# A linear-attention layer and a balanced mixture of experts: u spread over the partitions by TensorE, and one expert's second weights issued later

## The chip, the cores and the metric

The kernel runs on one core of one Trainium2 chip. The metric is the device time of one execution in microseconds; lower is better. The kernel before takes 377.23 us (median of 3 runs, 376.42 to 378.08).

## The reference, cut to what matters

All data is float32. The first half is an attention with a decaying state (4 batches, 8 heads, 768 steps, 48 channels):

```python
for t in range(S):
    kt, vt, rt = k[:, :, t], v[:, :, t], r[:, :, t]
    cur = einsum('bhd,bhe->bhde', u[None] * kt, vt)
    y[:, :, t] = einsum('bhd,bhde->bhe', rt, state + cur)
    state = w[None, :, :, None] * state + einsum('bhd,bhe->bhde', kt, vt)
```

`u` and `w` hold 8 x 48 values; `u` weighs the step's own key and value. The outputs are laid out as 3072 rows of 384. The second half gives each row to one of 8 experts: all (row, expert) scores are sorted, and each expert takes its best 384 rows that are still free. Then, for each expert e,

```python
h = maximum(x[mask] @ w1[e], 0.0)      # w1[e]: 384 x 1024
out[mask] = h @ w2[e]                  # w2[e]: 1024 x 384
```

## The kernel before

The attention works in 24 units of 128 steps of one batch (unit n is chunk n // 4 of batch n % 4). Class `Mild` does it, and its method `run` issues everything in an order written out by hand; each engine executes its own part of that order, one instruction after the other, and waits on semaphores where data is missing. For a unit, TensorE turns keys and r (`keys_turned`, `r_turned`, from unit 2 on `turn`), VectorE scales them with powers of w (table W), TensorE multiplies keys with r (`pairs`, g_ps), and VectorE copies the masked result over a diagonal (AT). The diagonal holds the sum over channels of r·k·u: GpSimd multiplies r with k (`own_raw`, L435) and by u (`own_rest`, L440), VectorE sums (`own_sum`, dd, L444), ScalarE and VectorE put dd on the diagonals (`diagonal`). So u is needed with its 384 values on each of the 128 partitions, as u_bc. `outputs` then makes the unit's result, which is turned to rows and written to the internal tensor x_rows (L621) two units later.

Nearly all loads are issued by SyncE, in the order of the program, and go through one queue: in `start` w, keys and r of unit 0, u as a broadcast from memory to all partitions (L353), then keys, r and v of the next units. `idle` issues turnings of the identity that nobody reads.

While the last units run, one expert (the "star") is chosen from the chunks that are done, and its first 256 rows are listed among the first 20 units. The generator `walk.early` does this in eleven steps, and the list `steps` says at which place of which unit each is taken. Its third step, in unit 18, knows the expert and calls `on_star`, which loads both of its weight matrices; its tenth, in the middle of unit 23, has the row numbers (e_tok) and calls `on_tokens`, which issues two gathers of 128 rows from x_rows by GpSimd (L1531). A gather waits until the rows of units 0 to 19 have landed in memory.

After the last unit TensorE turns the gathered rows (e_xT_ps, L1898), multiplies them with w1 (e_h_ps, L1906) and later with w2 (e_o_ps, L1915). Between these products the choice of the next expert goes on: VectorE makes masks (ind) and TensorE counts with them (counts). The other experts follow, each with weights, gather, two products and a scatter, with a search for the next between.

Names in the rows: krs are keys and r of a unit (loaded from in_k_dram and in_r_dram), vts its v, kT_ps and rT_ps keys and r turned, krT the scaled ones, rk the product of r and k, xr a unit's rows before they are written, w the weights of an expert, xg gathered rows, spare_ps a free bank of PSUM.

Of the kernel before, what the change touches and what calls it, by code (L numbers as in the profile page):

```python
# [10 lines left out]
F32 = mybir.dt.float32  # L11
# [265 lines left out]
class Mild:  # L277
# [30 lines left out]
    def open(self, ctx):  # L308
        tc, HP, H, D, B = self.tc, self.HP, self.H, self.D, self.B
        const = self.const = ctx.enter_context(tc.tile_pool(name="m_const", bufs=1))  # L310
        self.pool = ctx.enter_context(tc.tile_pool(name="m_work", bufs=2))
        self.xpool = ctx.enter_context(tc.tile_pool(name="m_x", bufs=1))
        self.ps = ctx.enter_context(tc.tile_pool(name="m_ps", bufs=1, space=PSUM))
        self.NK, self.NV, self.NS = 5, 6, 3
        self.krs = const.tile([128, self.NK, 2, H, PD], F32, name="krs")
        self.vts = const.tile([128, self.NV, H, PD], F32, name="vts")
        self.kss = const.tile([128, self.NS, H, PD], F32, name="kss")
        self.states = const.tile([128, B, HP, PD], F32, name="states")
        self.wp = const.tile([128, HP], F32, name="wp")
        self.wc = const.tile([128, HP], F32, name="wc")  # L320
        self.ones8 = const.tile([128, 2, 2, HP, 9], F32, name="ones8")
        self.times = const.tile([128, HP, 9], F32, name="times")
        self.begin = const.tile([128, HP, 9], F32, name="begin")
        self.Q = const.tile([128, 2, HP, 9, 8], F32, name="Q")
        self.chunk = const.tile([128, HP], F32, name="chunk")
        self.W = const.tile([128, 2, HP, T], F32, name="W")
        self.WK, self.WR = self.W[:, 0], self.W[:, 1]
        self.wk = const.tile([128, H, D], F32, name="wk")
        self.u_bc = const.tile([128, H, D], F32, name="u_bc")
        self.wgp = const.tile([128, HP, 32], F32, name="wgp")  # L330
        self.mask_f = const.tile([128, T], F32, name="mask_f")
        self.mask = const.tile([128, T], U8, name="mask")
        self.bad = const.tile([128, HP], BF16, name="bad")
        self.xts, self.live, self.lgs, self.unscaled = {}, {}, {}, []

    def load(self, n, what):
        if n >= self.N:
            return
        nc, H, D = self.nc, self.H, self.D
        b, c = self.units[n]  # L340
        for x in what:
            t = self.vts[:, n % self.NV] if x == "v" else self.krs[:, n % self.NK, "kr".index(x)]
            src = {"k": self.k, "r": self.r, "v": self.v}[x]
            nc.sync.dma_start(t[:, :, 0:D], src[b, :, ts(c, T), :].rearrange("h s d -> s h d"))

    def start(self):
        nc, HP, H, D = self.nc, self.HP, self.H, self.D
        nc.vector.memset(self.wp, 1.0)
        with nc.allow_non_contiguous_dma(reason="a row to the partitions"):
            for z, eng in enumerate((nc.sync, nc.scalar)):  # L350
                eng.dma_start(self.wp[z * PD:z * PD + D, :], self.w[z:H:2].rearrange("h d -> d h"))
        self.load(0, "kr")
        nc.sync.dma_start(self.u_bc.rearrange("p h d -> p (h d)"), self.u.rearrange("h d -> (h d)").partition_broadcast(128))  # L353
        for n, what in ((1, "kr"), (0, "v"), (2, "kr"), (1, "v"), (3, "kr"), (2, "v"), (4, "kr"), (3, "v")):
            self.load(n, what)
        make_identity(nc, self.ident)
        nc.vector.memset(self.krs[:, :, :, :, D:PD], 0.0)
        AB = self.ones8
        nc.vector.memset(self.times[:, :, 0:1], 0.0)
        nc.vector.memset(self.begin, 0.0)  # L360
        nc.vector.memset(self.begin[:, :, 0:1], 1.0)
        nc.gpsimd.memset(self.wgp, 0.0)
        nc.scalar.copy(self.bad, self.ident[:, 0:HP])
        self.spare = self.ps.tile([128, 2, 512], F32, name="spare_ps", tag="y_ps")
        self.idle(12, self.spare[:, 1])

        nc.gpsimd.memset(self.mask_f, 1.0)
        nc.gpsimd.affine_select(out=self.mask_f, in_=self.mask_f, compare_op=ALU.is_ge, fill=0.0, base=-1,
                                pattern=[[1, T]], channel_multiplier=-1)
        nc.gpsimd.memset(self.kss[:, :, :, D:PD], 0.0)  # L370
        nc.gpsimd.memset(self.vts[:, :, :, D:PD], 0.0)
        nc.gpsimd.memset(self.states[:, :, :, D:PD], 0.0)
        nc.gpsimd.tensor_copy(self.mask, self.mask_f)


        def powers(i):
            nc.vector.tensor_tensor_scan(out=AB[:, 0, i].rearrange("p a j -> p (a j)"),
                                         data0=self.times.rearrange("p a j -> p (a j)"),
                                         data1=self.begin.rearrange("p a j -> p (a j)"),
                                         initial=0.0, op0=ALU.mult, op1=ALU.add)  # L380

        each = self.times[:, :, 1:9]
        nc.vector.tensor_scalar(out=each, in0=self.wp.unsqueeze(2).to_broadcast([128, HP, 8]), scalar1=W_MIN,
                                scalar2=W_MAX, op0=ALU.max, op1=ALU.min)
        powers(0)
        nc.vector.tensor_copy(each, AB[:, 0, 0, :, 8:9].to_broadcast([128, HP, 8]))
        powers(1)
        nc.vector.reciprocal(AB[:, 1], AB[:, 0])
        for x, eng in ((0, nc.gpsimd), (1, nc.vector)):
            eng.tensor_mul(self.Q[:, x], AB[:, x, 1].unsqueeze(3).to_broadcast([128, HP, 9, 8]),  # L390
                           AB[:, x, 0, :, 0:8].unsqueeze(2).to_broadcast([128, HP, 9, 8]))
        self.own_raw(0)
        Q = self.Q.rearrange("p x a i j -> p x a (i j)")
        M = PD
        self.pieces = {"k": ((slice(0, M + 1), Q[:, 0, :, M::-1]), (slice(M + 1, T), Q[:, 1, :, 1:T - M])),
                       "r": ((slice(0, M + 2), Q[:, 1, :, M + 1::-1]), (slice(M + 2, T), Q[:, 0, :, 1:T - M - 1]))}

    def gate_weights(self):
        wg = self.wg.rearrange("(i j z d) e -> i z d j e", i=2, z=2, d=self.D)
        for q in range(2):  # L400
            for i in range(2):
                self.nc.sync.dma_start(self.wgp[q * PD:q * PD + self.D, 2 * i:2 * i + 2, 0:self.E],
                                       wg[i, 1 - q if i else q])

    def idle(self, m, ps):
        if isinstance(ps, str):
# [234 lines left out]
    def run(self, step):  # L641
        N, B, C, walk = self.N, self.B, self.C, self.walk
        self.live = {n: {} for n in range(N)}
        self.start()
        k0 = self.keys_turned(0, True)
        r0 = self.r_turned(0)
        self.own_rest(0)
        self.scaled(0, "k", k0, "pieces")
# [2 lines left out]
        self.table(self.WR, "r")  # L651
        self.own_sum(0)
        self.diagonal(0, (1,), self.spare[:, 1, 0:T])
        self.idle(2, "g_ps")
        k1 = self.keys_turned(1, True, walk.ps, "few")
        self.scaled(1, "k", k1, self.WK)
        self.pairs(0)
# [5 lines left out]
        nc, AB = self.nc, self.ones8  # L663
# [80 lines left out]
        last = self.rows_turned((N - 1,), "g_ps")  # L744
# [720 lines left out]
def rwkv5_eagle_then_base_layer_balanced(  # L1465
# [12 lines left out]
    nc = tc.nc  # L1478
# [21 lines left out]
    class Experts:  # L1500
# [11 lines left out]
            self.first = pool("f_first", 1, **how)  # L1512
            self.ps_t, self.ps_h, self.ps_o = (pool(f"f_ps_{x}", 2, space=PSUM, **how) for x in "tho")

        def load_weights(self, n, fmax):
            number = walk.outs.tile([1, 1], I32, name="number")
            nc.vector.tensor_scalar(out=number, in0=fmax[0:1, :], scalar1=1.0, scalar2=float(E),
                                    op0=ALU.max, op1=ALU.min)
            pool = self.turns[n % 2]
            w1, w2 = pool.tile([128, KD, F], F32, name="w1"), pool.tile([128, KF, DX], F32, name="w2")  # L1520
            e = nc.values_load(number[0:1, 0:1], engines=(mybir.EngineType.SP,), min_val=1, max_val=E,
                               skip_runtime_bounds_check_because="held between 1 and E")
            for t, src in ((w2, moe_w2), (w1, moe_w1)):
                nc.sync.dma_start(t, src[ds(E - e, 1)].rearrange("o (c p) f -> p (o c) f", p=128))
            return w1, w2

        def gather(self, n, tok, within=N):
# [395 lines left out]
    with ExitStack() as whole:  # L1923
        x = Experts()
# [3 lines left out]
        have = {}  # L1928
        first = walk.new_outs()
        with ExitStack() as part:  # L1930
# [2 lines left out]
            epool = part.enter_context(tc.tile_pool(name="f_early", bufs=1))  # L1933

            def on_star(star):
                have["w"] = x.load_weights(0, star)

            def on_tokens(tok):
                have["x"] = x.gather(0, tok, N - N // C), tok
# [2 lines left out]
            U = mild.N  # L1942
# [4 lines left out]
            def step(n, at):  # L1947
                for _ in range(steps.count((n, at))):
                    next(early)

            with tc.manual_schedule():
                one, last = mild.run(step)
# [24 lines left out]
                second = walk.new_outs()  # L1977
# [55 lines left out]
    with tc.If(have["ok"] < 1, label="whole", preferred_fallthrough_block=False):  # L2033
# [3 lines left out]
        with ExitStack() as arm:  # L2037
            x = Experts()
# [40 lines left out]
```

## Time and profile before

| | |
|---|---|
| median of 3 runs | 377.23 us (376.42 to 378.08) |
| the profiled execution | 378.76 us |
| its span, first to last instruction | 377.0 us |
| mean granted TensorE clock | 0.998 |
| TensorE busy (matmul / weight load) | 96% / 79% of the span |
| VectorE, ScalarE, GpSimd busy | 75%, 47%, 36% |
| moved by DMA | 60.74 MB, 161 GB/s on average |

The rows further down come from this profiled execution. Its span and the 1.76 us around it make its time. A busy TensorE is not one at its peak, and time in which an engine stands still matters only where something behind it is late for that reason.

### The profile page before, as it was taken

The numbers are of one execution on the slowest core, as the hardware profiler recorded it, in microseconds if no ns is written. First come the engines' busy times: TensorE is split into PE (matmuls) and PEld (weight loads), VectorE is DVE, ScalarE is ACT, GpSimd is POOL, SyncE is SP. The second block draws the span as 40 slices with busy tenths as digits, with TensorE's granted clock in tenths as the row PEclk, the third lists the DMA queues.
The fourth block names the chain that finished last, engine by engine and source line by source line (L and its number), as shares of the span: only waits on it lengthen the run. The fifth ranks groups of instructions, "written<-read, shape, count | busy, mean of one in ns | idle before, by whom it ended". The sixth has DMA issues, their size and how long they took to land.

```text
span 377.0 us, 10330 instructions
## 1 busy us (share of the span) xinstructions
PE 360.3 (96%) x4008; PEld 298.7 (79%) x4008; DVE 283.1 (75%) x945; ACT 177.2 (47%) x457; POOL 136.8 (36%) x169
## 2 busy tenths in 40 slices
PE   6889999999998999999999999999999999999994
PEld 5678888888786757587997898559657889989994
DVE  5888899789984677976978869877367964995640
ACT  3787878888753202234435444321222535535230
POOL 6898987787402041212112121103203422060031
PEclk9999999999999999999999999999999999999999
DMA  6998878888793091825646463109109574590110
GB/s 127 196 185 192 188 170 188 191 182 184 207 325 108 12 383 45 314 87 103 229 190 107 155 265 83 43 7 367 67 23 324 156 252 188 81 381 23 24 64 29
DMA packets 108234, 60.74 MB, mean 161 GB/s; under 512 B 90000, under 2 KB 102416, under 8 KB 108176
## 3 DMA queue, kind: packets, MB, share of 16 engines
q1 hardware_dynamic: 104896, 50.55, 49.3%
q0 software_dynamic: 3072, 9.44, 7.1%
q8 instruction: 33, 0.54, 0.7%
q14 instruction: 25, 0.20, 0.2%
q10 hardware_dynamic: 208, 0.00, 0.0%
HBM read 47.40 MB, written 9.44 MB: 151 GB/s over the span
## 4 chain that ended last, share of the span: by engine, by line
PE 51%; DMA 17%; issue 15%; DVE 11%; POOL 3%; SPq 2%; POOLq 0%; ACT 0%; DVEq 0%
DMA out_dram<-o_all,to 9%; PE y_ps L556 6%; PE o_ps L1801 6%; PE h_ps L1656 5%; PE pa_ps L1730 5%; PE g_ps L516 4%; PE h_ps L1633 4%; PE hb_ps L1633 3%; DMA xg<-x_rows,tok 3%; DMA w<-in_moe_w_dram 3%; PE e_h_ps L1906 3%; DVE AT L523 2%; PE kr_ps L488 2%; PE kv_ps L535 2%; DVE krT L492 2%
## 5 line engine op out<-in xcount | busy, mean ns | idle before, releaser
L506 ACT ACTIVATE AT<-ident,dd 128x128 f32<-128x128 f32 x188 | 58.3, 394 | 6.4 <-DVE dd L444 6.4
L1656 PE MATMUL h_ps<-xT,w 128*128 128x384 f32 (+1 forms) x216 | 56.3, 412 | 0.5 <-ACT xT L1547 0.5
L1785 POOL DMA_INDIRECT out_dram<-o_all,to x16 | 21.5, 1346 | 89.8 <-DVE o_all L1773 41.0
L1531 POOL DMA_INDIRECT xg<-x_rows,tok x22 | 22.3, 1015 | 85.1 <-DVE own_c L1457 31.6
L1656 PEld LDWEIGHTS h_ps<-xT,w 128*128 128x128 f32 x216 | 33.3, 191 | 14.4 <-issue 1.3
L523 DVE COPY_PREDICATED AT<-mask,g_ps 64x512 f32<-64x512 uint8 (+1 forms) x48 | 32.4, 725 | 3.5 <-PE g_ps L516 1.5
L1659 ACT ACTIVATE hid<-h_ps 128x384 f32<-128x384 f32 (+1 forms) x32 | 14.0, 437 | 42.7 <-PE h_ps L1656 41.0
L492 DVE TENSOR_TENSOR krT<-kr_ps,W 112x512 f32<-112x512 f32 x44 | 28.1, 679 | 3.3 <-PE kr_ps L488 3.3
L435 POOL TENSOR_TENSOR rk<-krs 128x384 f32<-128x384 f32 x24 | 24.3, 1012 | 13.9 <-DMA krs<-in_r_dram 6.5
L1801 PE MATMUL o_ps<-w,hid 128*128 128x384 f32 x80 | 28.0, 491 | 0.0
L516 PE MATMUL g_ps<-krT 48*64 48x128 f32 (+1 forms) x768 | 26.3, 255 | 1.7 <-DVE AT L523 1.0
L556 PE MATMUL y_ps<-AT,vts 128*64 128x128 f32 x384 | 25.7, 276 | 0.0
L440 POOL TENSOR_TENSOR rk<-rk,u_bc 128x384 f32<-128x384 f32 x24 | 24.2, 1007 | 3.1 <-DMA u_bc<-in_u_dram 1.3
L516 PEld LDWEIGHTS g_ps<-krT 48*64 48x64 f32 x768 | 20.6, 132 | 3.7 <-PE kv_ps L535 1.1
L556 PEld LDWEIGHTS y_ps<-AT,vts 128*64 128x64 f32 x384 | 20.6, 137 | 1.1 <-issue 0.9
L1621 ACT ACTIVATE hid<-kept_P 128x384 f32<-128x384 f32 x24 | 12.6, 523 | 17.4 <-DVE kept_P L1625 17.1
L1801 PEld LDWEIGHTS o_ps<-w,hid 128*128 128x128 f32 x80 | 14.5, 190 | 7.7 <-issue 0.4
L426 POOL TENSOR_TENSOR kss<-krs,wk 128x384 f32<-128x384 f32 x20 | 20.3, 1017 | 0.0
L620 ACT COPY xr<-x_ps 128x192 f32<-128x192 f32 x48 | 12.9, 324 | 8.0 <-PE x_ps L606 3.8
L575 ACT COPY x<-y_ps 128x512 f32<-128x512 f32 x24 | 14.0, 583 | 4.3 <-PE y_ps L556 3.6
L556 PE MATMUL y_ps<-krT,states 48*64 48x128 f32 x320 | 15.8, 278 | 0.2 <-ACT x L575 0.2
L488 PE MATMUL kr_ps<-ident,krs 64*112 64x64 f32 x352 | 15.0, 223 | 0.9 <-DVE krT L492 0.3
(337 smaller groups left out, 838.1 us busy)
## 6 DMA issues: line engine op xcount, KB each, us to landing
w<-in_moe_w_dram SPq DMA_DIRECT2D x18, 1536.0 KB, 9.2
krs<-in_k_dram SPq DMA_DIRECT2D x24, 192.0 KB, 4.2
krs<-in_r_dram SPq DMA_DIRECT2D x24, 192.0 KB, 4.4
vts<-in_v_dram SPq DMA_DIRECT2D x24, 192.0 KB, 4.8
x_rows<-xr SPq DMA_DIRECT2D x24, 192.0 KB, 4.3
xg<-x_rows,tok POOLq DMA_INDIRECT x22, 5.3
xg<-xg SPq DMA_TRANSPOSE x16, 3.4
out_dram<-o_all,to POOLq DMA_INDIRECT x16, 3.3
```

The costliest lines, as they stand in the source:

```text
L435: nc.gpsimd.tensor_mul(rk, self.krs[:, n % self.NK, 1, :, 0:D], self.krs[:, n % self.NK, 0, :, 0:D])
L440: self.nc.gpsimd.tensor_mul(rk, rk, self.u_bc)
L488: nc.tensor.transpose(ps[0:P, x, a, :], self.pair(kr[:, x], a)[rows], self.ident[rows, rows])
L492: nc.vector.tensor_mul(t[0:P, :, :, ts(i, PD)], ps[0:P], self.W[0:P, :, :, ts(i, PD)])
L506: nc.scalar.mul(AT[:, z, a, :], self.ident, dd[:, h:h + 1])
L516: nc.tensor.matmul(g_ps[ts(i, PD), z, a, i * PD:], kT[rows, a, ts(i, PD)], rT[rows, a, i * PD:], start=True, stop=True)
L523: nc.vector.copy_predicated(out=AT[keys, :, :, steps], mask=mask, data=g_ps[keys, :, :, steps])
L556: nc.tensor.matmul(yv[q * PD:(q + 1) * PD, o // 2, o % 2, :], lhsT, rhs, start=(o // 2, q) not in seen, stop=stop, skip_group_check=True)
L1531: self.gathered = nc.gpsimd.indirect_dma_start(out=xg[:, c, :], out_offset=None, in_=x_dram[0:within, :], in_offset=bass.IndirectOffsetOnA ...
L1633: nc.tensor.matmul(ps[:, q, :], w[b][:, ts(p * Q + q, 128)], x[a], start=fresh, stop=(a, b) == pairs[-1], skip_group_check=True)
L1656: nc.tensor.matmul(h_ps[j][:, at], w1[:, f, ts(j, 128)], xT[:, f, at], start=(f == 0), stop=(f == KD - 1))
L1801: nc.tensor.matmul(o_ps, hid[:, j, ts(c, 128)], w2[:, j, :], start=(j == 0), stop=(j == KF - 1))
```

## The change

Two things are changed.

u no longer comes as a broadcast from memory. ScalarE's queue loads it as a column tile u_col of 128 x 3 values. `spread_u` then issues three turnings on TensorE: its operand is one column of u_col, read 128 times by a step of zero, so that each turning puts 128 values of u on all partitions. ScalarE copies the 384 columns from PSUM to u_bc. The turnings stand between the keys and the r of unit 0. Two unread turnings a little later are left out.

The star's weights are no longer loaded together. `on_star` loads w1 alone; w2 is issued in unit 23 after the last of the eleven steps, so that in the program it stands behind the two gathers. All other experts load w2 and then w1, as before.

```diff
@@ start @@
-        self.load(0, "kr")
-        nc.sync.dma_start(self.u_bc.rearrange("p h d -> p (h d)"), self.u.rearrange("h d -> (h d)").partition_broadcast(128))
-        for n, what in ((1, "kr"), (0, "v"), (2, "kr"), (1, "v"), (3, "kr"), (2, "v"), (4, "kr"), (3, "v")):
+            nc.scalar.dma_start(self.u_col, self.u.rearrange("h d -> (h d)").rearrange("(c p) -> p c", p=128))
+        for n, what in ((0, "kr"), (1, "kr"), (0, "v"), (2, "kr"), (1, "v"), (3, "kr"), (2, "v"), (4, "kr"), (3, "v")):
             self.load(n, what)
...
+    def spread_u(self):
+        nc, ps = self.nc, self.spare[:, 0, 0:self.H * self.D]
+        for c in range(self.H * self.D // 128):
+            nc.tensor.transpose(ps[:, ts(c, 128)], self.u_col[:, c:c + 1].to_broadcast([128, 128]), self.ident)
+        nc.scalar.copy(self.u_bc.rearrange("p h d -> p (h d)"), ps)
@@ run @@
         k0 = self.keys_turned(0, True)
+        self.spread_u()
         r0 = self.r_turned(0)
...
         self.diagonal(0, (1,), self.spare[:, 1, 0:T])
-        self.idle(2, "g_ps")
         k1 = self.keys_turned(1, True, walk.ps, "few")
@@ load_weights @@
-            for t, src in ((w2, moe_w2), (w1, moe_w1)):
+            def load(t, src):
                 nc.sync.dma_start(t, src[ds(E - e, 1)].rearrange("o (c p) f -> p (o c) f", p=128))
+            if later:
+                load(w1, moe_w1)
+                return w1, w2, lambda: load(w2, moe_w2)
+            load(w2, moe_w2)
+            load(w1, moe_w1)
             return w1, w2
@@ on_star, step @@
-                have["w"] = x.load_weights(0, star)
+                *have["w"], have["second"] = x.load_weights(0, star, later=True)
...
                 for _ in range(steps.count((n, at))):
                     next(early)
+                if (n, at) == (U - 1, "last"):
+                    have["second"]()
```

How the order of instructions changes, at two places. First TensorE at the start of the program, before (spare_ps here takes the unread turnings; kT_ps and rT_ps are those of unit 0, then of unit 1):

```order
L409 MATMUL spare_ps_186<-ident_58 128x128 x12
L453 MATMUL kT_ps_214<-ident_58,krs_135 112x128 x4
L453 MATMUL rT_ps_219<-ident_58,krs_135 112x128 x4
L409 MATMUL unread_ps_242<-ident_58 128x128 x2
L453 MATMUL kT_ps_245<-ident_58,krs_135 112x128 x4
```

and TensorE at the same place now:

```order
L415 MATMUL spare_ps_187<-ident_58 128x128 x12
L459 MATMUL kT_ps_215<-ident_58,krs_135 112x128 x4
L408 MATMUL spare_ps_187<-ident_58,u_col_149 128x128 x3
L459 MATMUL rT_ps_224<-ident_58,krs_135 112x128 x4
L459 MATMUL kT_ps_247<-ident_58,krs_135 112x128 x4
```

The three turnings of u stand before those of r(0), and the two unread ones are gone.

Second SyncE from unit 18 on, before, from the rows of unit 16 on (w2 and w1 are the star's weights, the five transfers from xr_2366 on are those of units 17 to 21):

```order
L621 DMA x_rows<-xr_2252 128x384
L1521 TENSOR_LOAD number_2293
L1524 ISA
L1524 DMA w2_2296<-in_moe_w2_dram 128x8x384
L1524 ISA
L1524 DMA w1_2295<-in_moe_w1_dram 128x3x1024
L344 DMA vts_136<-in_v_dram 128x8x48
L621 DMA x_rows<-xr_2366 128x384
L621 DMA x_rows<-xr_2470 128x384
L621 DMA x_rows<-xr_2589 128x384
L621 DMA x_rows<-xr_2669 128x384
L621 DMA x_rows<-xr_2732 128x384
```

and SyncE at the same place now:

```order
L1530 DMA w1_2297<-in_moe_w1_dram 128x3x1024
L345 DMA vts_136<-in_v_dram 128x8x48
L627 DMA x_rows<-xr_2367 128x384
L627 DMA x_rows<-xr_2471 128x384
L627 DMA x_rows<-xr_2590 128x384
L627 DMA x_rows<-xr_2670 128x384
L627 DMA x_rows<-xr_2733 128x384
L1530 ISA
L1530 DMA w2_2298<-in_moe_w2_dram 128x8x384
L627 DMA x_rows<-xr_2812 128x384
L627 DMA x_rows<-xr_2816 128x384
```

w2 has moved behind the rows of unit 21 and ahead of those of the last two units.

## Rows read from the trace of the kernel before

**Rows 1.** The page's chain of waits, by engine: share of the span.

```profile
PE 51%; DMA 17%; issue 15%; DVE 11%; POOL 3%; SPq 2%; POOLq 0%; ACT 0%; DVEq 0%
```

**Rows 2.** Timeline of GpSimd, 4 to 9 us: start us, us, instruction, [idle before it, releaser].

```profile
5.44 1.03 POOL L435 TENSOR_TENSOR rk<-krs 128x384 f32<-128x384 f32 x1 [0.51 <-DMA krs<-in_r_dram]
7.75 1.00 POOL L440 TENSOR_TENSOR rk<-rk,u_bc 128x384 f32<-128x384 f32 x1 [1.28 <-DMA u_bc<-in_u_dram]
```

**Rows 3.** Timeline of SyncE at the start: the load of u.

```profile
2.54 0.72 SPq L353 DMA_DIRECT2D u_bc<-in_u_dram  x1
```

**Rows 4.** DMA issues in two stretches at the start: KB each, us to landing.

```profile
wp<-in_w_dram ACTq DMA_DIRECT2D x1, 0.8 KB, 2.2
...
u_bc<-in_u_dram SPq DMA_DIRECT2D x1, 192.0 KB, 5.1
```

**Rows 5.** Timeline of VectorE, 4 to 10 us.

```profile
6.49 0.76 DVE L468 TENSOR_TENSOR krT<-rT_ps,Q 112x264 f32<-112x264 f32 x2 [0.23 <-PE rT_ps L453]
8.78 0.55 DVE L444 TENSOR_REDUCE dd<-rk 128x8 f32<-128x384 f32 x1 [1.54 <-POOL rk L440]
```

**Rows 6.** Timeline of TensorE's matmuls, 1 to 13 us.

```profile
4.32 1.07 PE L453 MATMUL kT_ps<-ident,krs 128*112 128x128 f32 x4
5.35 1.10 PE L453 MATMUL rT_ps<-ident,krs 128*112 128x128 f32 x4
...
8.40 0.66 PE L453 MATMUL kT_ps<-ident,krs 128*112 128x128 f32 x4 [1.52 <-DMA krs<-in_k_dram]
```

**Rows 7.** Chain of waits, 0 to 32 us: start us, us, what.

```profile
8.34 3.72 DMA krs<-in_r_dram
...
16.33 1.00 POOL rk L440
```

**Rows 8.** Chain of waits, 111.9 to 119.9 us.

```profile
111.95 0.16 DVE e_tok L1448
...
114.19 0.63 POOL xg L1531
...
115.68 3.11 DMA xg<-x_rows,e_tok
```

**Rows 9.** DMA issues at 108 us: the rows of unit 19.

```profile
x_rows<-xr SPq DMA_DIRECT2D x1, 192.0 KB, 5.2
```

**Rows 10.** Timeline of TensorE, then of VectorE, 107 to 121 us.

```profile
116.51 0.33 PE L596 MATMUL lt_ps<-ident,lg 128*128 128x128 f32 x1
...
118.83 0.55 PE L1898 MATMUL e_xT_ps<-ident,xg 128*128 128x128 f32 x3 [0.77 <-DMA xg<-x_rows,e_tok]
...
119.66 0.25 PE L950 MATMUL counts<-prop,ind 128*128 128x64 bf16 x3
...
118.23 0.35 DVE L927 TENSOR_TENSOR ind<-at,from_digit 128x384 bf16<-128x384 int16 x1
```

**Rows 11.** Timeline of ScalarE, 0 to 14 us.

```profile
4.96 1.36 ACT L413 COPY W<-Q 128x260 f32<-128x260 f32 x4 [2.04 <-POOL Q L390]
...
11.13 0.48 ACT L422 COPY wk<-spare_ps 128x384 f32<-128x384 f32 x1 [0.48 <-PE spare_ps L418]
```

**Rows 12.** Timeline of VectorE, then of GpSimd, 134.5 to 135.3 us: the next gather.

```profile
134.79 0.17 DVE L1448 TENSOR_REDUCE tok<-mine 128x3 int32<-128x12 f32 x1
...
135.23 0.94 POOL L1531 DMA_INDIRECT xg<-x_rows,tok  x1 [18.60 <-DVE own_c L1457]
```

**Rows 13.** Timeline of ScalarE, 110 to 120 us: the copy of unit 21's rows.

```profile
112.31 0.54 ACT L620 COPY xr<-x_ps 128x192 f32<-128x192 f32 x2 [0.58 <-DMA x_rows<-xr]
```

**Rows 14.** DMA issue at 130.2, and a window row: us, busy, clock, DMA share, GB/s.

```profile
w<-in_moe_w_dram SPq DMA_DIRECT2D x1, 1536.0 KB, 6.9
...
131.17:132.17 1.00, 1.00 (x4) 0.57 (x3) 0.97 (x5) 0.30 (x1) 0.00 (x0) 1.00 0.78 118
```

**Rows 15.** The gathers' line, in the stretches 135 to 139 and 187 to 190.

```profile
DMA to landing us min/median/max: 4.7/5.4/6.0
...
DMA to landing us min/median/max: 5.3/6.0/7.0
```

More of the change, by code (lines that the diff above doesn't have):

```diff
@@ L329, in open @@
         self.u_bc = const.tile([128, H, D], F32, name="u_bc")
+        self.u_col = const.tile([128, H * D // 128], F32, name="u_col")
         self.wgp = const.tile([128, HP, 32], F32, name="wgp")
@@ L1513, in open_rest, with load_weights @@
             self.ps_t, self.ps_h, self.ps_o = (pool(f"f_ps_{x}", 2, space=PSUM, **how) for x in "tho")
-        def load_weights(self, n, fmax):
+        def load_weights(self, n, fmax, later=False):
             number = walk.outs.tile([1, 1], I32, name="number")
```

## The prediction

> **What bounds the kernel now.** I read the page's chain of waits first: TensorE carries half of it, DMA a sixth [rows 1]. So the kernel is a long TensorE program, and a change pays only where that program stands still and something the change touches ends the standstill. The timelines show two such places.
>
> The first is the opening 20 us. The reader should see GpSimd waiting 1.28 us, from 6.47 to 7.75, for the broadcast of u [rows 2], while the load of u is one of the early issues on SyncE [rows 3] and lands 5.1 us later [rows 4]. VectorE's sum of r·k·u (dd) can only follow, at 8.78 [rows 5], and the diagonals, the masked copy and everything of the next units stand behind it. TensorE waits 1.52 us for the keys of unit 1, whose load is queued behind u [rows 6]. The chain of this stretch runs over the load of r(2), which lands at 12.06, and then over GpSimd to 17.33 [rows 7].
>
> The second is 112 to 120 us. The early expert's token list is ready at 112.11, the first gather starts at 114.19, and the second lands at 118.79 [rows 8]. The chain puts VectorE's work in front of the gather, but the transfer of unit 19's rows, which the gather reads, was issued at 108.01, takes 5.2 us and lands near 113.2 [rows 9]: it is queued behind two loads of expert weights, 1.5 MB each. TensorE is done with the attention part at 116.84 and stands still before both turnings of gathered rows, 0.77 us before the second [rows 10].
>
> **Start, step by step.** Removed: one 192 KB broadcast on SyncE and two unread turnings. Added: one load of 3 values to each of 128 partitions on ScalarE's queue, three 128x128 turnings on TensorE between keys and r of unit 0, and one 128x384 copy on ScalarE ahead of the four copies of the W table.
> - u_col. Its nearest row is w's load on the same queue, 192 pieces of 4 bytes in 2.2 us [rows 4]; u_col has 384. Issued at about 1.4, it lands between 3.6 and 6.5 (the 5.1 us of the broadcast). I take 4.5, nearer to w: TensorE then doesn't wait for it, since the keys' turning ends at 5.39 [rows 6].
> - Turnings. Four take 1.07 us here and 0.66 us at 8.40 [rows 6]. I take the longer: three add 0.80 us, from 5.35 to 6.15. The turning of r(0) then moves from 5.35 to 6.15 and its scaling on VectorE ends not at 7.25 [rows 5] but near 7.9 to 8.0, the two unread turnings behind it being gone, which nobody waited for.
> - Copy. A 128x384 copy from PSUM took 0.48 us [rows 11]: u_bc stands at about 6.7. The W copies, 1.36 us from 4.96 [rows 11], move to 6.7 to 8.1; their first reader on VectorE stands behind dd, which ends at 8.45 at the earliest, so that work hides them.
> - GpSimd multiplies by u at 6.75 instead of 7.75 and ends near 7.8. dd then waits for r(0)'s scaling: 7.9 instead of 8.78. **Term: -0.85 us.**
> - It holds only if the loads follow. The SyncE issue of u (0.72 us) [rows 3] and its 192 KB go, so r(2) should come earlier by something between 0.7 us and the 2.3 us from r(0)'s arrival (about 5.3, [rows 6]) to u's (7.6); the chain needs 0.85 of it.
> - Ends: the best is GpSimd's whole wait, -1.28; the worst is u_col landing at 6.5, which puts r(0)'s scaling near 9.0 and costs +0.25.
>
> After 20 us I see no absolute date that could eat this: the chain returns to TensorE and VectorE, and loads were shifted as well.
>
> **Gather, step by step.** w2 (1.5 MB) is no longer ahead of the rows of units 17 to 21. With only w1 in front, unit 19's rows land before 112, so the gather waits for its token list alone: in the later pair of rows the list is finished at 134.96 and the gather starts at 135.23 [rows 12], so 112.11 + 0.27 = 112.4 instead of 114.19. The second follows 1.49 us later, at 113.9.
>
> What is new: nothing but program order ties w2 to the gather. SyncE issues it right after unit 21's rows. Their copy on ScalarE lost 0.58 us waiting for an older rows transfer [rows 13], which now lands early; so those rows go out at 112.3 (112.31 - 0.58 + 0.54) and w2, one SyncE issue of 0.72 later, at about 113.0, 0.9 us ahead of the second gather. The two transfers queued behind w2 are the rows of the last two units, needed by the gather at 135: covered. w2 itself lands near 113.0 + 6.9 = 119.9 [rows 14], when TensorE is at the first of the products that come before its first use: covered.
>
> So the second gather shares the engines with w2. Alone it took 3.11 us [rows 8]. Beside weights, the three gathers behind the first weights took 4.7/5.4/6.0, and the worst of seven such groups 5.3/6.0/7.0 [rows 15]. There the weights were well under way; a weight load moves only 118 GB/s in its second microsecond [rows 14], and here the gather is issued just then. I take 4.3 us, between the 3.1 alone and the median 5.4 of the group behind the first weights: it lands at 118.2 instead of 118.79. Rows 15 against rows 8 say that a gather beside weights loses 1.6 to 3.9 us. The Trainium skill (DMA: Bandwidth & Descriptors, Queues, rings and completion order) says that each engine takes turns between its queues packet by packet; by that alone sharing would cost the second gather at most its own moving time again, an estimated 1 us, and the sum would be 0.2 us better. The rows are worse than that rule, so it changes no bound.
>
> How much of an early landing counts? TensorE is free at 116.84 and would turn the first block until 117.4 (0.55 us, as the second); the first counting product stands behind the second block and four products and needs the mask that VectorE ends at 118.58 [rows 10]. It ran at 119.66, so the most to be had is 119.66 - 118.62 = 1.04 us. Term: 118.79 - 118.2 = 0.59, less a little handing over, **-0.55 us**; ends -1.04 (landing by 117.5) and +2.1 (landing 7.0 us after 113.9). From there TensorE is full until the next token list, so it carries through.
>
> **Sum.** 378.76 us is the profiled execution, 377.0 its span and 1.76 what lies around it. 378.76 - 0.85 - 0.55 = 377.36. That execution was 1.53 above the median of 377.23, so against the median: 377.23 - 1.40 = **375.8 us**.
>
> **Rivals.**
> - Both in full: u lands early, the keys' loads follow, w2 stays slow until the gather is through: -1.28 - 1.04, so 374.9. For it: SyncE's queue loses a whole broadcast and the 1.52 us wait of TensorE goes too. Against: the three turnings stand in front of r(0).
> - The gather doesn't gain: the second takes the 5.4 us median beside weights and lands at 119.3. -0.85 + 0.5 = -0.35, so 376.9. For it: w2 is issued before it, not behind. Against: w2's slow first 2 us.
> - Slower: w2 collides with the second gather as in the worst group. The place is the turning of the second block on TensorE, the price 7.0 - 3.1 = 3.9 us less the 1.8 that the gather starts earlier: +2.1. It decides from a landing of 119.64 on (118.79 + 0.85), that is 5.7 us after issue. 377.23 - 0.85 + 2.1 = 378.5, and with u_col at its late end 379.6.
> - The change doesn't do what it says: that is the second and third case, w2 "behind" the gather in the program and ahead of it on the queue.
>
> **How the numbers follow.** Forecast 0.45 (own range 375.2 to 376.4), both in full 0.26, no gain at the gather 0.20, slower 0.09. The range of 8 in 10 reaches from somewhat under the second case to somewhat over the third: 374.5 to 377.4. A measurement of this kernel tells about 0.5% from no change, which is 1.9 us: faster means under 375.3, slower over 379.1. Faster takes most of the second case and a tenth of the first, 0.30; slower takes half of the last case, 0.05; the rest, 0.65, is no difference.
>
> **What would show it.** GpSimd's first product with u near 6.75 without a wait for a DMA; dd near 7.9; r(2) no later than 11.2; the same lead of 0.8 to 0.9 at about 20 and at 110 us. Then, in the time of before less that lead: first gather 0.3 us after its list, w2's issue before the second gather, the second landing about 0.6 earlier, TensorE's wait there under 1 us. I am wrong if u's turnings wait for u_col, if r(2) has not moved by 0.85, if the lead of the start is lost before 110, or if the second gather lands later than before.

## The result and the profile after

The changed kernel takes 381.15 us (median of 5 runs, 379.78 to 382.04) where the kernel before takes 377.23: ratio 1.011, 95% interval 1.0093 to 1.0128. It is slower by 1.1%. The prediction was 375.8 us, with 374.5 to 377.4 as its range of 8 in 10, and it was wrong. The profiled execution has a span of 378.0 us (before 377.0). It is the fastest of the five and has the mildest clock, 0.995; the others had 0.991 to 0.984. So the trace shows only a part of the 3.9 us between the medians.

The start moved about as far as forecast. GpSimd, VectorE and TensorE (start us, us, instruction, [idle before it, releaser]):

```profile
6.80 1.00 POOL L446 TENSOR_TENSOR rk<-rk,u_bc 128x384 f32<-128x384 f32 x1 [0.45 <-ACT u_bc L409]
...
7.83 0.55 DVE L450 TENSOR_REDUCE dd<-rk 128x8 f32<-128x384 f32 x1 [0.46 <-POOL rk L446]
...
5.52 0.62 PE L408 MATMUL spare_ps<-ident,u_col 128*128 128x128 f32 x3
...
16.11 1.10 PE L522 MATMUL g_ps<-krT 48*64 48x128 f32 x32 [1.83 <-DVE AT L529]
```

The product with u starts at 6.80 instead of 7.75 [rows 2], dd at 7.83 instead of 8.78 [rows 5]. dd waits there for GpSimd's product, and not for the scaling of r(0), which the prediction had last. Before the products of unit 2 (last row) TensorE now stands 1.83 us. In the kernel before it stood 1.03 us there, and the products came 0.93 us later:

```profile
17.04 1.10 PE L516 MATMUL g_ps<-krT 48*64 48x128 f32 x32 [1.03 <-DVE AT L523]
```

The chain there no longer runs over a load and GpSimd [rows 7] but over ScalarE's diagonals of unit 1:

```profile
12.14 2.46 ACT AT L512 x8
...
15.25 0.72 DVE AT L529
```

The gather is where the time went. Chain of waits, 108 to 124 us, then the issue of w2 on SyncE's timeline, then the DMA issues from 110 to 113 us (KB each, us to landing):

```profile
110.01 0.16 DVE e_tok L1454
...
110.46 1.18 POOL xg L1543
...
111.95 6.61 DMA xg<-x_rows,e_tok
```

```profile
110.91 0.40 SPq L1530 DMA_DIRECT2D w<-in_moe_w_dram  x1
```

```profile
w<-in_moe_w_dram SPq DMA_DIRECT2D x1, 1536.0 KB, 8.3
...
xg<-x_rows,e_tok POOLq DMA_INDIRECT x2, 6.9
```

The token list is 1.94 us earlier than before [rows 8] and the first gather follows 0.3 us behind it. But w2 goes out at 110.91, 0.45 us after the first gather and 1.04 ahead of the second. The second gather takes 6.61 us where it took 3.11 [rows 8], and the first takes 7.1 where it took 3.3. TensorE's matmuls there, then its windows (us, busy of the five engines with counts, granted clock, DMA share, GB/s):

```profile
117.60 0.55 PE L1910 MATMUL e_xT_ps<-ident,xg 128*128 128x128 f32 x3 [2.41 <-DMA xg<-x_rows,e_tok]
118.61 0.90 PE L1910 MATMUL e_xT_ps<-ident,xg 128*128 128x128 f32 x3 [0.46 <-DMA xg<-x_rows,e_tok]
...
120.15 0.37 PE L956 MATMUL counts<-prop,ind 128*128 128x64 bf16 x3
120.33 1.85 PE L1918 MATMUL e_h_ps<-xT,w 128*128 128x128 f32 x8
...
124.29 0.25 PE L956 MATMUL counts<-prop,ind 128*128 128x64 bf16 x3
```

```profile
116.00:118.00 2.00, 0.40 (x3) 0.31 (x3) 0.89 (x4) 0.00 (x0) 0.00 (x0) 1.00 1.00 361
118.00:120.00 2.00, 1.54 (x9) 1.40 (x8) 0.00 (x0) 0.94 (x3) 0.00 (x0) 0.60 0.09 30
120.00:122.00 2.00, 2.00 (x13) 1.94 (x13) 1.25 (x5) 0.91 (x5) 0.00 (x0) 0.54 0.34 125
```

TensorE waits 2.41 and 0.46 us, and after that the granted clock is at its lower level, 1.2 of 2.4 GHz, for most of 118 to 122 us: eight products take 1.85 us. The same eight, and the count behind them, in the kernel before:

```profile
119.75 1.14 PE L1906 MATMUL e_h_ps<-xT,w 128*128 128x128 f32 x8
...
123.07 0.25 PE L950 MATMUL counts<-prop,ind 128*128 128x64 bf16 x3
```

So the first counting product comes 0.49 us later than before [rows 10], and the second 1.22 (124.29 - 123.07): a lead of 1.94 us has become a lag of 1.22 within 14 us. Of that lag about 1 us is left at the end. From the start of the second block's turning to that second count it is 5.68 us against 4.24: in this execution the half clock costs 1.44 us.

### The profile page after: what moved, and what is told of

Its sections match the earlier page's. It is cut to its first block, busy times and chain, and to the rows that moved or that the text cites. A ratio compares the mean times of both kernels' runs of the same rounds, so it can differ in the third digit from the quotient of the medians.

```text
span 378.0 us, 10335 instructions
## 1 busy us (share of the span) xinstructions
PE 360.5 (95%) x4009; PEld 299.7 (79%) x4009; DVE 282.7 (75%) x945; ACT 177.5 (47%) x458; POOL 136.6 (36%) x169
## 4 chain that ended last, share of the span: by engine, by line
PE 62%; DMA 16%; DVE 9%; issue 8%; POOL 1%; ACT 1%; POOLq 0%; SPq 0%; DVEq 0%
DMA out_dram<-o_all,to 9%; PE h_ps L1668 9%; PE y_ps L562 7%; PE pa_ps L1742 6%; PE o_ps L1813 6%; PE g_ps L522 5%; PE h_ps L1645 4%; PE hb_ps L1645 3%; PE e_h_ps L1918 3%; PE kr_ps L494 3%; DMA w<-in_moe_w_dram 3%; PE pb_ps L1742 3%; PE kv_ps L541 3%; DVE AT L529 2%; DMA xg<-x_rows,e_tok 2%
## 5 line engine op out<-in xcount | busy, mean ns | idle before, releaser
L1776 PE MATMUL p_ps<-W,H 128*128 128x128 f32 x128 | 15.3, 275 | 0.0
```

## The experiments

Kernels of one group ran on one chip and share its runs of the kernel before: median 378.88 us for the first four, 377.94 for the next four, 379.56 for the last. Between groups only ratios are compared.

**The u part alone.**

```diff
-                *have["w"], have["second"] = x.load_weights(0, star, later=True)
+                have["w"] = x.load_weights(0, star)
...
-                if (n, at) == (U - 1, "last"):
-                    have["second"]()
```

> u as a column with its three turnings, but both weight matrices of the early expert loaded together as in the kernel before. Theory A (the whole loss comes from the moved w2, which delays the gathers until TensorE stands 2.4 us and its clock falls; the new start is a gain of the 0.93 us read at 20 us in the trace after): 376.3 us, 375.8 to 376.8, full granted clock at 118 to 122. Theory B (the earlier start itself shifts the work so that the clock falls, w2 or not): 380 to 381.5 us with a stretch at half clock.

378.06 us, ratio 0.9983 (0.9966 to 0.9999). In its trace the gain is larger, span 375.5 us, and TensorE does not wait for the gathers at all:

```profile
115.82 0.82 PE L1910 MATMUL e_xT_ps<-ident,xg 128*128 128x128 f32 x6
...
117.78 0.26 PE L956 MATMUL counts<-prop,ind 128*128 128x64 bf16 x3 [0.20 <-DVE ind L933]
```

The first counting product is 1.88 us earlier than before [rows 10], with w2 still ahead of w1. SyncE issues both in one go at 94.01, in the first profile of the kernel before at 98.89:

```profile
94.01 1.02 SPq L1530 DMA_DIRECT2D w<-in_moe_w_dram  x2
```

```profile
98.89 1.02 SPq L1524 DMA_DIRECT2D w<-in_moe_w_dram  x2
```

In this execution there was nothing left for the second part to gain. That the earlier start is what cleared the queue is not shown: in the second profile of the kernel before, further down, the gather does not wait for the rows either.

**The later w2 alone**, with u as a broadcast and the two unread turnings as before.

> u broadcast from memory and two unread turnings as in the kernel before; only w2 is issued late. Theory A: the loss without the start's gain, so 381.15 + 0.93 = about 382.1 us (380.5 to 382.5), gathers landing 6 to 7 us after their issue and half clock from about 118. Theory B: no loss without the earlier start, 376.5 to 377.5 us.

383.33 us, ratio 1.0114 (1.0079 to 1.0148): the whole loss. TensorE waits twice for the gathers and then runs at the lower clock:

```profile
119.90 0.55 PE L1911 MATMUL e_xT_ps<-ident,xg 128*128 128x128 f32 x3 [1.45 <-DMA xg<-x_rows,e_tok]
121.49 0.90 PE L1911 MATMUL e_xT_ps<-ident,xg 128*128 128x128 f32 x3 [1.04 <-DMA xg<-x_rows,e_tok]
```

```profile
122.00:124.00 2.00, 2.00 (x12) 1.94 (x11) 0.51 (x2) 1.37 (x5) 0.00 (x0) 0.50 0.00 0
```

The lower clock, seen here from 121 to 127.7 us, lasts longer than in the kernel after, and this execution also ran at half clock from 8 to 15 us: the size of the loss differs from execution to execution.

**Both, with w2 behind the rows of the last two units.**

```diff
-                if (n, at) == (U - 1, "last"):
-                    have["second"]()
...
                 mild.rows_out((U - 1,), last)
+                have["second"]()
```

> The changed kernel with w2's load moved further back, behind the rows of the last two units; SyncE then waits for their copies, which stand behind the turning of the gathered rows, so w2 cannot start before the gathers have landed. Theory A: gathers take 3.1 to 3.3 us, TensorE waits under 0.5 us for them, clock full; 377.23 - 0.93 (start) - 0.8 (units 18 to 23 with w1 alone) - 1.0 (earlier gather) = 374.5 us, 373.8 to 375.3. If lateness of w2 itself costs (it is needed for the products at about 128 us and lands near 125): a wait of TensorE before those products, 376 to 378. Theory C (the clock falls for another reason than the gathers' delay): 380 us.

378.11 us, ratio 0.9975 (0.9954 to 0.9996): the loss is gone, but the 1.8 us that were expected on top of the start are not there: against the u part alone nothing is gained. In its profiled execution the clock fell elsewhere, right after the longer stand before unit 2:

```profile
16.32 1.98 PE L522 MATMUL g_ps<-krT 48*64 48x128 f32 x32 [1.83 <-DVE AT L529]
```

```profile
16.00:18.00 2.00, 1.68 (x32) 1.61 (x32) 0.88 (x3) 2.00 (x8) 1.65 (x3) 0.59 0.86 169
```

The same 32 products take 1.98 us instead of 1.10. Of the 12 runs the seven with a mean clock of 0.995 or more have a median of 377.54 us, the other five 379.55. In the runs of the u part alone clock and time go together less: one with a clock of 1.000 took 379.25 us.

**After, with TensorE kept busy before the gathered rows.**

```diff
+                mild.idle(13, walk.ps.tile([128, T], F32, name="unread_ps", tag="few"))
                 go(NE)
```

> The changed kernel with 13 unread turnings (about 2.1 us) on TensorE between the last logits and the turning of the gathered rows; w2 still collides with the gathers. Theory A with the clock as the price: gathers land at 117.6 and 118.6 as in the changed kernel, but the clock stays full, so the first counting product comes at about 119.4 instead of 120.15 and nothing is lost behind it: 376.8 us, 376.3 to 377.6. Theory D (the lateness of the gathers is the price, the clock is not): 380 to 381 us, as the changed kernel.

379.94 us, ratio 1.0034 (1.0013 to 1.0056).

```profile
116.66 1.64 PE L415 MATMUL unread_ps<-ident 128*128 128x128 f32 x13 [0.28 <-ACT LG L603]
118.13 0.49 PE L1910 MATMUL e_xT_ps<-ident,xg 128*128 128x128 f32 x3
119.19 0.55 PE L1910 MATMUL e_xT_ps<-ident,xg 128*128 128x128 f32 x3 [0.56 <-DMA xg<-x_rows,e_tok]
```

The gathers are as late as in the kernel after, the clock stays at 1.00 in this execution, and a good part of the loss goes. So both theories hold a part. From the u part alone (0.9983) to here it is 0.51%, 1.9 us: the price of the late gathers. From here to the kernel after (1.011) it is 0.76%, 2.9 us: what the turnings took away. I put that down to the clock. In the one trace of the kernel after the clock costs 1.44 us; its other executions have lower mean clocks and no trace, and those of this run go down to 0.988. So the split is a rough one.

**The kernel before, profiled again.**

> The kernel before, profiled a second time. The u part alone saved 1.95 us by its trace and only about 0.7 us by its times. First reading: the wait of TensorE for the second gather (0.77 us, first counting product at 119.66) belongs to every execution of the kernel before; then it is here again within 0.3 us. Rival: it belongs to that one execution; then the first counting product is here at 119.0 or earlier with no wait before the second turning of gathered rows, and the u part has less to save there than the first trace says.

378.79 us, span 377.0 as in the first profile, but with the time lost in another place:

```profile
117.64 1.03 PE L1898 MATMUL e_xT_ps<-ident,xg 128*128 128x128 f32 x6
...
119.61 0.26 PE L950 MATMUL counts<-prop,ind 128*128 128x64 bf16 x3 [0.15 <-DVE ind L927]
```

```profile
8.00:10.00 2.00, 1.65 (x20) 1.30 (x24) 1.23 (x3) 0.68 (x3) 1.51 (x2) 0.50 0.96 186
```

The weights and the first gather here:

```profile
96.92 1.02 SPq L1524 DMA_DIRECT2D w<-in_moe_w_dram  x2
```

```profile
113.35 1.18 POOL L1531 DMA_INDIRECT xg<-x_rows,e_tok  x1 [13.12 <-DVE good L927]
```

The weights go out 1.97 us earlier than in the first profile, with nothing changed, and the gather starts 0.3 us behind its list (ready at 113.06). The wait for the gather on which the second term was built belonged to one execution. That the count comes at 119.61 all the same, and not by 119.0, is due to the half clock in the first 15 us, after which this execution was 0.8 us behind the first one.

**The u part with the stand before unit 2 filled.**

```diff
                     self.keep(n - 1)
+                    if n == 1:
+                        self.idle(10, walk.ps.tile([128, T], F32, name="unread_ps", tag="few"))
                     self.pairs(n + 1)
```

> The u part alone, and ten unread turnings (1.3 us by 13 of them in 1.64 us) in TensorE's stand of 1.83 us before the products of keys and r of unit 2. Theory: with u early TensorE stands there longer than before (1.03 us), and in part of the executions the clock falls to half there, as in the trace of the kernel with w2 behind the last rows (16.36 to 23.19 us, some 3.2 us lost). Filled, no execution shows it: ratio 0.994 to 0.996, clocks 0.995 or more in all runs. Rival: the clock at the start plays no part in the u part's small gain: 0.998, as without the turnings.

376.50 us, ratio 0.9964 (0.9951 to 0.9977), clocks of 0.996 to 1.000 in all 11 runs; without the turnings they were 0.991 to 1.000.

```profile
13.86 1.31 PE L415 MATMUL unread_ps<-ident 128*128 128x128 f32 x10
15.77 1.10 PE L522 MATMUL g_ps<-krT 48*64 48x128 f32 x32 [0.60 <-DVE AT L529]
```

The turnings cost nothing, as they end before the data comes. The interval overlaps that of the u part alone, so the gain from filling is not clear by the times of this pair. The clock is: u is early and the stand filled in three kernels (this one and two further down), and none of their 24 runs is under 0.996. None of their three traces falls to half clock at the start, where three of the seven with the stand unfilled do, as after 16.36 us above.

**After, with w2 in two halves.**

```diff
-                return w1, w2, lambda: load(w2, moe_w2)
+                s2 = moe_w2[ds(E - e, 1)].rearrange("o (c p) f -> p (o c) f", p=128)
+                half = KF // 2
+                return (w1, w2, lambda: nc.sync.dma_start(w2[:, 0:half], s2[:, 0:half]),
+                        lambda: nc.sync.dma_start(w2[:, half:KF], s2[:, half:KF]))
```

> The kernel after, with w2 in two halves: the first (0.75 MB) where the change put it, the second behind the rows of the last two units. Theory 1: what delays the gathers is the bytes that are on the engines beside them; half the bytes, about half the delay: the second gather lands some 2.5 us after its issue plus half of the 3.5 us that it lost, and the ratio is 1.002 to 1.006. Theory 2: it is the issue of any large load between the two gathers, whatever its size: both gathers take over 6 us and the ratio stays at 1.009 to 1.013. Rival: half is hidden altogether, ratio 0.998.

380.35 us, ratio 1.0072 (1.0045 to 1.0098), between the two expectations. Its issues, 110 to 113 us:

```profile
w<-in_moe_w_dram SPq DMA_DIRECT2D x1, 768.0 KB, 5.9
...
xg<-x_rows,e_tok POOLq DMA_INDIRECT x2, 6.0
```

With half the bytes the first gather still takes 6.6 us and the second 5.5. TensorE waits 1.89 us for them and then runs at half clock for 3.4 us. The queues show more. Here is the stretch from 1.5 to 3 us after the first gather's issue (packets, MB, share of 16 engines; q0 is the gathers' queue, q1 that of SyncE), for the kernel before, the kernel after, the halves, and the filled u part:

```profile
q0 software_dynamic: 64, 0.20, 49.0%
```

```profile
q1 hardware_dynamic: 170, 0.26, 87.8%
```

```profile
q1 hardware_dynamic: 166, 0.25, 75.4%
```

```profile
q0 software_dynamic: 61, 0.19, 49.9%
q1 hardware_dynamic: 9, 0.01, 3.3%
```

Beside w2, whole or half, no packet of a gather moves in that stretch; without it half of the 0.39 MB of both gathers has moved. By the trace's packets the first comes 1.9 us after the issue in the kernel before and the filled one, 4.1 us in the kernel after (114.54), 4.2 us in the halves. That late start is 2.2 of the 3.8 us that the first gather loses in the kernel after, and it is the same with half the size. Once under way the gathers do share, in the kernel after from 114.5 to 116 us:

```profile
q1 hardware_dynamic: 261, 0.40, 71.4%
q0 software_dynamic: 58, 0.18, 32.8%
```

The Trainium skill (DMA: Bandwidth & Descriptors, Queues, rings and completion order) has each engine take turns between its queues by packets. The last two rows, with 71.4% and 32.8%, agree with that. The stretch before, in which one queue had all, cannot tell: whether the gathers' packets were not yet there, or there and not taken, no row shows.

**After, with w2 issued by GpSimd behind both gathers.**

```diff
-            e = nc.values_load(number[0:1, 0:1], engines=(mybir.EngineType.SP,), ...
+            e = nc.values_load(number[0:1, 0:1], engines=(SP, Pool) if later else (SP,), ...
...
-                return w1, w2, lambda: load(w2, moe_w2)
+                return w1, w2, lambda: nc.gpsimd.dma_start(w2, moe_w2[ds(E - e, 1)]...)
```

> The kernel after, with w2 issued by GpSimd instead of SyncE, so that it comes after both gathers on their own engine (some 0.1 us behind the second, near 113.0 us). Theory 1 (order): a gather is delayed only by a load issued before its own first packets; here the first gather takes about 3.2 us and the second at most 4.5, TensorE waits under 0.5 us, ratio 0.998 to 1.000. Theory 2 (sharing): the second gather runs beside w2 all the same and takes 6 us or more, TensorE waits for it 1.5 us or more, and the clock falls in part of the executions: ratio 1.004 to 1.010.

381.23 us, ratio 1.0065 (1.0037 to 1.0092), as the theory of sharing had it; but the profile says otherwise. Issues from 115 to 119 us, then GpSimd and TensorE around 95 us:

```profile
w<-in_moe_w_dram POOLq DMA_DIRECT2D x1, 1536.0 KB, 8.3
...
xg<-x_rows,e_tok POOLq DMA_INDIRECT x2, 3.5
```

```profile
95.33 1.00 POOL L441 TENSOR_TENSOR rk<-krs 128x384 f32<-128x384 f32 x1 [9.74 <-DVE states L546]
```

```profile
98.42 0.79 PE L541 MATMUL kv_ps<-vts,kss 128*64 128x48 f32 x16 [1.89 <-POOL kss L432]
```

The gathers take 3.5 us and TensorE does not wait for them. The loss is one of the edit: GpSimd stood 9.74 us in unit 18, where it now reads the expert's number, TensorE waited 1.89 us behind it, and the clock was at half for 3.4 us from 98.8 us on. This execution had another such stretch from 16.9 us on, behind the stand before unit 2. The next run takes the reading out of unit 18.

**The same, with GpSimd reading the number only behind the gathers.**

```diff
+                def second():
+                    e = nc.values_load(number[0:1, 0:1], engines=(mybir.EngineType.Pool,), ...
+                    nc.gpsimd.dma_start(w2, moe_w2[ds(E - e, 1)]...)
```

> As the run with w2 issued by GpSimd behind both gathers, but GpSimd reads the expert's number only there, and not in unit 18, where it stood 9.74 us for it and made TensorE wait 1.89 us at 96.5 us, after which the granted clock was 0.5 for 3.4 us. Theory (order): w2 behind both gathers costs nothing; gathers of 3 to 4.4 us, no wait of TensorE for them, no half clock after 95 us, ratio 0.996 to 0.999. Rival (sharing): the 1.0065 of that run was due to w2 beside the second gather; then the ratio stays at 1.004 or more.

378.67 us, ratio 0.9978 (0.9959 to 0.9996). GpSimd issues both gathers and then w2, and TensorE turns all six blocks without a wait:

```profile
112.12 1.18 POOL L1548 DMA_INDIRECT xg<-x_rows,e_tok  x1 [13.14 <-DVE good L933]
...
114.55 0.96 POOL L1538 DMA_DIRECT2D w<-in_moe_w_dram  x1
```

```profile
117.55 0.82 PE L1915 MATMUL e_xT_ps<-ident,xg 128*128 128x128 f32 x6
```

Here w2 goes out at 114.55, 2.4 us behind the first gather and 0.95 behind the second, and costs nothing. In the kernel after it went out 0.45 us behind the first. But w2 is now also in the gathers' own queue, and by the trace's packets the last one of the gathers starts at 116.10 and the first one of w2 at 116.24: the two never moved side by side. So the run shows that w2 is harmless behind the gathers in their queue. It does not separate the order from the queue, and it says nothing on sharing. A w2 that SyncE issues 2.4 us behind the gather would tell; no run has that.

**Both parts, w2 behind the last rows, the stand filled** (the edits of the third and the sixth run together).

> Both parts with w2 behind the rows of the last two units, and the ten unread turnings in front of the products of unit 2. Theory: the later w2 adds nothing, since with u early the gathers land before TensorE is free in either order; the turnings take the half clock away: 0.995 to 0.998, like the u part with the turnings (0.9964). Rival: w2 out of the way of the rows and the gathers is worth something of its own, 0.992 to 0.994.

378.03 us, ratio 0.9959 (0.9944 to 0.9974): as the filled u part. The later w2 adds nothing.

**The kernel before, filled.**

```diff
-        self.idle(2, "g_ps")
+        self.idle(8, "g_ps")
...
+                    if n == 1:
+                        self.idle(6, walk.ps.tile([128, T], F32, name="unread_ps", tag="few"))
```

> The kernel before with unread turnings in its two stands at the start: eight instead of two before the keys of unit 1 (it stood 1.52 us there, and in the second profile the granted clock was 0.5 from 7.8 to 14.6 us), six before the products of unit 2 (1.03 us). Theory 1: the gain of the u part with turnings is u's, some 1 us, plus the clock's where before lost it too: here 0.997 to 0.999. Theory 2: all of the gain is the clock at the start and u is worth nothing: 0.996. Rival: turnings at half clock delay the keys of unit 1 by up to 1 us, 1.000 to 1.003.

379.35 us, ratio 0.9996 (0.9981 to 1.0011). Turnings alone give nothing, although the mean clocks are higher with them (0.995 to 1.000, without them 0.987 to 0.999 on the same chip). So the gain of the filled kernels needs u. The profiled execution still had a stretch of half clock, from 23.25 us on, after a stand of 1.62 us.

**The filled u part with the two unread turnings back.**

```diff
         self.diagonal(0, (1,), self.spare[:, 1, 0:T])
+        self.idle(2, "g_ps")
         k1 = self.keys_turned(1, True, walk.ps, "few")
```

> The u part with the ten turnings before unit 2, and the two unread turnings that the change leaves out put back. Theory: they stand where TensorE waits 0.4 us for scaled keys anyway; 0.996 to 0.997, and the same clocks. Rival: they were needed for the clock, or cost up to 0.5 us.

377.17 us, ratio 0.9938 (0.9925 to 0.9951), the fastest by ratio; better than expected, with clocks of 0.997 to 1.000 in its six runs. Whether the two turnings themselves help is open: its interval and that of the sixth run, from another chip, touch at 0.9951, and on the same chip the filled kernel with both parts, without the two, has 0.9959. Either version beats both kernels.

## Why the prediction was wrong

- **The start.** Right in size: -0.85 said, 0.95 measured at dd. The u_col load, the turnings and the copy came nearly as worked out. The last wait was another: dd waited for GpSimd's product and not for the scaling of r(0). The forecast had the two 0.1 us apart, so it was luck that this did not show. No absolute date ate the lead before the token list; against the first profile it had even grown to 1.94 us there, and why is not shown. What the step left out is what comes next on the path: ScalarE's diagonals, a stand of 1.83 us on TensorE, and the clock that falls there in some executions. With it the u part is worth 0.17%, filled 0.4 to 0.6%.
- **The gather: the step that failed.** "I take 4.3 us" for the second gather; it took 6.6. So the term forecast at -0.55 us came out as a loss, 1.14% for the later w2 alone. And I let only the second share with w2, while the first, issued ahead of w2, was hit as well: its packets start 1.9 us after its issue when nothing follows, w2 came in between, and they started at 4.1. The worst of the seven groups [rows 15] comes nearest, for both. I argued from w2's slow second microsecond [rows 14], and that did not protect the gather.
- **The gain was not there either.** The term counted on a wait of TensorE in the trace of before [rows 10]. The second profile of the kernel before has no such wait, nor has the u part alone. With w2 out of the gathers' way the later w2 is worth nothing on top of u (0.9975 against 0.9983; filled, 0.9959 against 0.9964). I had charged the wait to the weights ahead of unit 19's rows [rows 9]. In the second profile the weights stand ahead of these rows just as well, and the gather starts 0.3 us behind its list. The order of the queue alone does not make the wait.
- **The price of the standstill.** No case had TensorE stand 2.4 and 0.5 us and then run at half clock. By the run with TensorE kept busy that is up to 2.9 of the 4.8 us (1.27%) between the u part alone and the kernel after. The rival "slower" had the right place, and the collision with the second gather, but 378.5 us and a chance of 0.09. It lacked the clock: with 2.9 us more it comes to 381.4, near the 381.15 measured.
- **What stays open.** Why a gather's first packets wait behind a load issued just after it on another queue: the runs show the times of issue and the 2.2 us, not the mechanism. Nor is it shown how far behind the gather such a load must be issued to do no harm.

## What to carry to other kernels

Program order between two issuing engines is no order at the queues: compare the times at which they issue. Here a large load 0.45 us behind a gather, on another queue, held up the gather's first packets; issued from the gather's own engine behind it, or once the gathers had landed, it did no harm. Price a standstill of TensorE with the clock that may follow, and where a stand can't be removed, try a few turnings that nobody reads. Before a wait is counted as a gain, see it in a second profile of the kernel before, and run each part of a change alone.

## What the runs showed of the hardware that was not expected

- Two gathers of 128 rows take 3.3 and 3.1 us in the first profile of the kernel before, with no weight load beside them (4.2 and 3.2 in the second), 7.1 and 6.6 when a load of 1.5 MB is issued 0.45 us behind the first on SyncE's queue, and 6.6 and 5.5 with 0.75 MB. The first packet comes 1.9 us after the issue without the load, 4.1 and 4.2 us with it. With w2 behind both in their own queue TensorE did not wait.
- The granted clock fell from 1.00 to 0.50 after stands of TensorE of 2.41 and 0.46 us with three turnings between them, and in some executions after a single one of 1.83 us. In others, with the same stand, it did not, as in the kernel after at 16.11 us, and it did not after 1.52 us in the first profile of the kernel before [rows 6].
